# A linear-attention layer and a feed-forward layer in one kernel: weight transfers tied to loads, two small inputs spread by TensorE, filler matmuls, and a new instruction order

## The chip, the cores and the metric

The kernel runs on one core of a Trainium2 chip. The metric is the device time of one execution in microseconds (us); the median over the runs is compared. Profiles are of single executions, and their span runs from the first to the last instruction of the program.

## The reference: what is computed

Four sequences of 768 steps with 8 heads of width 48 go through a recurrence, and its output goes through a feed-forward layer.

```python
for t in range(S):                       # S = 768, per batch b and head h
    cur = outer(u * k[t], v[t])
    y[t] = r[t] @ (state + cur)          # state is 48 x 48
    state = w[:, None] * state + outer(k[t], v[t])
x = y.transpose(0, 2, 1, 3).reshape(3072, 384)
h = x @ w_in                             # 384 x 2048
g = where(h >= 1, h, where(h <= -1, 0, (h + 1) ** 2 / 4))
out = g @ w_out                          # 2048 x 384
```

All inputs and the output are float32. `w` and `u` have 8 x 48 entries.

## The kernel before, in words

**Units and blocks.** The recurrence is cut into chunks of 128 steps. Six chunks times four sequences give 24 *units*; unit `i` is chunk `i // 4` of sequence `i % 4`. Two units make one *block* of 256 rows for the feed-forward layer, 12 blocks in all.

**One unit of the attention part.** Three loads bring K, R and V of the unit, each 128 x 384 float32 (L250, on SP's queue, tokens `ld:K:i` and so on). K and R are scaled by powers of `w` into one tile RKW (`Kw:i`, `Rw:i`, L254). The tile is transposed, for units 0 to 7 by TensorE (`trp:i`, L278, with the copy `trc:i`), for the others by a transposing DMA on SP's queue (`tr:i`, L287). Scores follow on TensorE (`at:i`, L294) and are masked on VectorE (`mk:i:s`, L298). The diagonal term needs K times u times R (`KU1:i` L262, `KU2:i` L265), a row sum (`dg:i`, L269) and, for units 0 to 5, V times that sum (`VD:i`, L273). `Vb:i` is V in bf16. `y:i` (L306 to L315) is the output in PSUM, `x:i` its copy, `xs:i` a sum of squares of it (L344), and `xp:i` its transposition, by TensorE for units 0 to 7 (L334, then the copy `xT:i`) and by DMA otherwise (L340). `st:i` (L350) is the unit's contribution to the state; `Ta`, `Td` and `Tb` (L356, L358, L361, L180) add, decay and cast the state. The decay uses the column vector `wc`.

**One block of the feed-forward part.** `L1:m:n` (L373) is six matmuls of 256 columns, 0.66 us; blocks 0 and 1 are worked unit by unit instead (`L1:m:n:u`, twelve matmuls of 128 columns, 0.67 us) so that they can begin with one finished unit. `sm:m:n` (L384, ScalarE) applies the quadratic. `L2:m:u:n` (L400) is two matmuls of 384 columns, 0.33 us. `oc:m:u` copies the result out of PSUM and `so:m:u` stores it (L415, SP's queue).

**Weights.** `w_in` and `w_out` are cast from float32 to bf16 while they are loaded, so POOL issues them, each in four quarters: `gi:q` (L422) and `go:q` (L425). `li:q` and `lo:q` stand for their landings. `L1` with index `n` of blocks 0 and 1 needs quarter `n` of `w_in`; `L2` with index `n` needs quarter `n // 2` of `w_out`.

**The order.** A string `ORDER`, found by a search ahead of time, lists every operation once as a token. The program walks through it and emits each operation on its engine, so the string fixes the order within every engine and within every DMA queue; nothing is reordered across a wait. A token `KU2:3@DVE` overrides the engine. The durations in the `op(...)` table were used by the search; in the kernel itself only the engine, the emitting function and the choice count.

**Small inputs.** `u` is loaded into all 128 rows by a broadcast DMA (L228), `w` likewise (L225), and `wc` by two DMAs of single words (L233), which stand in SP's queue between `ld:R:1` and `ld:K:2`.

Of the kernel before, what the change touches and what calls it, by code (L numbers as in the profile page):

```python
# [16 lines left out]
w ld:K:0 u gi:0 ld:R:0 ln tab:K ld:K:1 tab:R Kw:0 ld:V:0 gi:1 ld:V:1 Rw:0 li:0 trp:0 gi:2 trc:0 KU1:0 at:0  # L17
KU2:0 li:1 mk:0:1 gi:3 mk:0:0 dg:0 Vb:0 ld:R:1 VD:0 st:0 Kw:1 y:0 wc x:0 li:3 KU1:1 xs:0 xp:0 Rw:1 xT:0 dec
KU2:1 trp:1 Ta:0:1 L1:0:0:0 ld:K:2 trc:1 Ta:0:0 Vb:1 dg:1 L1:0:1:0 ld:R:2 VD:1 sm:0:0:0 st:1 go:1 sm:0:1:0
Ta:1:1 at:1 li:2 Ta:1:0 L1:0:3:0 Tb:0:1 Kw:2 mk:1:0 Tb:0:0 Tb:1:1 mk:1:1 sm:0:3:0 KU1:2 Tb:1:0 ld:V:2 Rw:2  # L20
y:1 KU2:2 x:1 ld:R:3 xs:1 trp:2 go:0 dg:2 L1:0:2:0 ld:K:3 trc:2 xp:1 Vb:2 ld:V:3 sm:0:2:0 VD:2 go:3 xT:1
at:2 ld:K:4 st:2 mk:2:1 go:2 L1:0:1:1 ld:V:4 Ta:2:0 L1:0:0:1 Rw:3 sm:0:1:1 lo:0 Kw:3 Ta:2:1 Tb:2:0 L1:0:2:1
mk:2:0 sm:0:0:1 KU1:3 Tb:2:1 L1:0:3:1 sm:0:2:1 y:2 Kw:4 ld:R:4 trp:3 x:2 trc:3 KU2:3@DVE ld:R:5 dg:3 KU1:4
xp:2 L2:0:1:0 sm:0:3:1 lo:1 L2:0:0:0 Rw:4 L2:0:0:1 xT:2 L2:0:1:1 Vb:4 xs:2 at:3 KU2:4 L1:1:0:0 mk:3:1 trp:4
ld:K:5 VD:3 sm:1:0:0 L1:1:2:0 mk:3:0 Vb:3 trc:4 ld:V:5 L1:1:1:0 dg:4 sm:1:2:0 st:4 VD:4 ld:R:6 y:3 Kw:5
Ta:4:1 sm:1:1:0 L2:0:1:2 Ta:4:0 at:4 ld:K:6 x:3 st:3 Rw:5 L1:1:3:0 xs:3 KU1:5 mk:4:0 ld:V:6 L2:0:0:2
sm:1:3:0 xp:3 Ta:3:1 L2:0:1:3 KU2:5 xT:3 mk:4:1 lo:2 L2:0:0:3 trp:5 Tb:3:1 Ta:3:0 Td:4 trc:5 dg:5 L1:1:0:1
Vb:5 y:4 VD:5 sm:1:0:1 lo:3 L1:1:2:1 Kw:6 x:4 at:5 Tb:4:1 Rw:6 sm:1:2:1 L1:1:1:1 mk:5:1 xs:4 xp:4 KU1:6
mk:5:0 st:5 L1:1:3:1 ld:R:7 xT:4 Ta:5:0 sm:1:1:1 trp:6 KU2:6 Ta:5:1 ld:K:7 y:5 sm:1:3:1 L2:0:0:4 Td:5 Tb:4:0
dg:6 ld:V:7 L2:0:1:4 x:5 Vb:6 L2:0:0:5 Tb:3:0 L2:0:1:5 trc:6 ld:R:8 L2:0:1:6 xp:5 st:6 Rw:7 L2:0:0:6 Ta:6:1  # L30
xT:5 ld:K:8 L2:0:0:7 Ta:6:0 L2:0:1:7 Tb:5:1 oc:0:0 Kw:7 at:6 Tb:5:0 ld:V:8 xs:5 oc:0:1 L1:2:0 Td:6 mk:6:0
L2:1:0:0 ld:K:9 sm:2:0 L2:1:0:1 KU1:7 mk:6:1 trp:7 ld:R:9 L1:2:2 KU2:7 trc:7 L1:2:4 ld:V:9 Vb:7 sm:2:2 y:6
dg:7 Vb:8 L2:2:1:0 Tb:6:0 x:6 so:0:0 L1:2:1 Kw:8 sm:2:4 so:0:1 at:7 sm:2:1 ld:R:10 L2:1:0:2 Rw:8 mk:7:1
Tb:6:1 st:7 L1:2:3 xs:6 ld:K:11 Ta:7:1 KU1:8 xp:6 Ta:7:0 sm:2:3 L2:1:0:3 mk:7:0 L2:1:0:4 ld:V:10 xT:6 KU2:8
L1:2:5 st:8 L2:1:0:5 sm:2:5 tr:8 Td:7 y:7 dg:8 Kw:9 L2:1:0:6 x:7 Tb:7:0 L2:1:0:7 Tb:7:1 ld:R:11 L1:2:6 Rw:9
L1:2:7 sm:2:6 ld:K:12 Ta:8:1 Vb:9 L2:2:1:1 oc:1:0 sm:2:7 xp:7 KU1:9 ld:K:10 Ta:8:0 L2:2:1:2 xs:7 L2:1:1:0
L2:1:1:1 Td:8 xT:7 ld:V:11 L2:1:1:2 KU2:9 L2:1:1:3 L2:1:1:4 L2:1:1:5 tr:9 L2:1:1:6 Vb:10 dg:9 at:8 Rw:10
L1:3:3 ld:R:12 mk:8:1 L1:3:0 Kw:10 sm:3:3 mk:8:0 ld:V:12 st:9 L2:1:1:7 sm:3:0 Ta:9:1 Rw:11 L2:2:1:3 oc:1:1
L1:3:1 ld:V:13 Ta:9:0 Kw:11 y:8 sm:3:1 so:1:0 L1:3:2 x:8 Tb:8:1 tr:10 Td:9 st:10 L1:3:4 sm:3:2 KU1:11 Tb:8:0
at:9 Ta:10:0 so:1:1 sm:3:4 L2:2:1:4 KU1:10@DVE ld:R:13 L1:3:5 xs:8 mk:9:1 KU2:10 L2:2:1:5 sm:3:5 ld:K:13  # L40
L1:3:6 mk:9:0 Vb:11 L2:2:1:6 Ta:10:1 sm:3:6 xp:8 L1:3:7 KU2:11 dg:10 y:9 sm:3:7 tr:11 L2:2:1:7 Td:10 x:9
st:11 Rw:12 oc:2:1@ACT at:10 Tb:9:0 L2:2:0:0 ld:K:14 Tb:9:1 L2:2:0:1 Kw:12 dg:11 L2:2:0:2 xs:9 L2:2:0:3
ld:R:14 mk:10:0 L2:2:0:4 KU1:12 L2:2:0:5 mk:10:1 L2:2:0:6 xp:9 L2:2:0:7 KU2:12 Ta:11:1 L2:3:1:0 oc:2:0
L2:3:1:1 ld:V:14 y:10 Vb:12 Ta:11:0 L2:3:0:0 x:10 Tb:10:0 Kw:13 L2:3:0:1 so:2:1 Tb:10:1 at:11 tr:12 L2:3:1:2
Vb:13 L2:3:0:2 Rw:13 mk:11:1 L2:3:0:3 xs:10 L2:3:1:3 so:2:0 mk:11:0 L2:3:1:4 ld:K:15 Rw:14 L2:3:0:4 st:12
dg:12 L2:3:0:5 L1:4:0 xp:10 Ta:12:1 Td:11 Ta:12:0 Kw:14 y:11 sm:4:0 ld:R:15 L1:4:1 x:11 Tb:11:1 Td:12 L1:4:2
sm:4:1 ld:V:15 KU1:14 L2:3:1:5 sm:4:2 L1:4:3 tr:13 KU1:13 Tb:11:0 at:12 sm:4:3 L1:4:4 mk:12:0 KU2:13 xs:11
xp:11 L1:4:5 mk:12:1 sm:4:4 KU2:14 L2:3:0:6 ld:K:16 dg:13 sm:4:5 L2:3:1:6 L1:4:6 Vb:15@ACT Vb:14 ld:R:16
dg:14 y:12 Rw:15 sm:4:6 L1:4:7 x:12 ld:V:16 Tb:12:0 L2:3:1:7 Kw:15 sm:4:7 L2:3:0:7 st:13 tr:14 st:14
oc:3:0@ACT oc:3:1 KU1:15 at:13 Tb:12:1 Ta:13:0 xs:12 L2:4:0:0 mk:13:1 ld:K:17 L1:5:0 KU2:15 mk:13:0 L2:4:1:0  # L50
sm:5:0 xp:12 L1:5:1 Kw:16 Ta:13:1 L2:4:1:1 Ta:14:1 sm:5:1 so:3:1 L1:5:2 Ta:14:0 Rw:16 dg:15 so:3:0 y:13
sm:5:2 ld:R:17 L2:4:0:1 Td:13 x:13 L1:5:3 Td:14 Tb:13:0 ld:V:17 L2:4:1:2 Vb:16 sm:5:3 at:14 Kw:17 L2:4:0:2
# [46 lines left out]
def kernel(  # L99
# [11 lines left out]
    nc = tc.nc  # L111
# [24 lines left out]

# [499 lines left out]
```

## Time and profile before

| | us |
|---|---|
| Median of 14 runs | 191.56 |
| Lowest and highest run | 190.12, 193.16 |
| The profiled execution's own time | 191.57 |
| Its span | 189.8 |
| TensorE busy | 161.3 |
| VectorE, ScalarE, GpSimd busy | 117.6, 108.1, 114.4 |

The profile's page has the busy time of each engine, the span in 40 slices, the DMA queues, the chain of waits that ended last, and the groups of instructions. Its names are PE for TensorE (PEld for its weight loads), DVE for VectorE, ACT for ScalarE, POOL for GpSimd and SP for the engine that issues most DMAs; "SPq" is SP's queue. `L254` is line 254 of the kernel. In a line of the timeline the two first numbers are the start and the duration in us, and a bracket at the end says how long the engine was idle before and what ended that. Matmuls overlap in the pipeline, so their busy time is a little more than what they cost.

### The profile page before, as it was taken

Reading aid. Unit: us, or ns where it says so; the run is one execution under the profiler, and the core shown is the slowest. Engines: PE = TensorE matmul, PEld = TensorE weight load, DVE = VectorE, ACT = ScalarE, POOL = GpSimd, SP = SyncE. Lnnn points to the kernel's source line nnn. Section 1 sums busy time; section 2 is a strip of 40 time slices with the busy share of each in tenths; the row PEclk is TensorE's granted clock in tenths of the full one; section 3 lists DMA queues with packets and bytes.
Section 4 is the critical chain, followed back from the end, with each engine's and each line's share of the span. In section 5 each row is a group of like instructions: output and inputs, shape, how many; then the busy total and the mean of one; then the engine's idle time right before and its main releaser. Section 6 shows DMA issues by size and latency. Waiting matters only on the chain.

```text
span 189.8 us, 4565 instructions
## 1 busy us (share of the span) xinstructions
PE 161.3 (85%) x1728; PEld 122.2 (64%) x1728; DVE 117.6 (62%) x312; ACT 108.1 (57%) x227; POOL 114.4 (60%) x151
## 2 busy tenths in 40 slices
PE   0214669789999999999999999998699999999980
PEld 0102648578877777667877767675477777777750
DVE  2240699698578568987886958959479746011210
ACT  3313475896978637439766576483876544643310
POOL 8744799099689898999988759883960000000000
PEclk9999996999999999999999999999999999999998
DMA  4999999999948999898989999989894112120031
GB/s 95 189 207 201 179 190 199 191 182 207 166 118 147 189 218 191 168 218 172 155 201 186 150 220 195 161 197 181 176 240 99 32 24 83 21 83 3 10 111 62
DMA packets 106476, 28.55 MB, mean 150 GB/s; under 512 B 99408, under 2 KB 106448, under 8 KB 106448
## 3 DMA queue, kind: packets, MB, share of 16 engines
q1 hardware_dynamic: 102592, 24.95, 68.1%
q0 software_dynamic: 3712, 3.15, 10.6%
q8 instruction: 15, 0.25, 0.5%
q14 instruction: 13, 0.11, 0.2%
q10 hardware_dynamic: 144, 0.10, 0.2%
HBM read 20.84 MB, written 4.72 MB: 135 GB/s over the span
## 4 chain that ended last, share of the span: by engine, by line
PE 60%; DMA 13%; DVE 9%; POOL 6%; SPq 5%; ACT 2%; issue 2%; ACTq 0%; DVEq 0%; POOLq 0%
PE o_p L400 26%; PE h_p L373 24%; DMA K<-in_k_dram 5%; DMA R<-in_r_dram 4%; POOL RKW L254 4%; DVE VD L273 4%; DMA wc<-in_w_dram 3%; PE A L294 3%; DVE AT L298 2%; PE y L309 2%; SPq L287 2%; PE y L306 1%; SPq L340 1%; PE tr L278 1%; DVE RKW L254 1%
## 5 line engine op out<-in xcount | busy, mean ns | idle before, releaser
L384 ACT ACTIVATE gT<-h_p 128x512 bf16<-128x512 f32 x96 | 56.9, 596 | 40.4 <-PE h_p L373 39.4
L373 PE MATMUL h_p<-xT,w_in_sb 128*128 128x256 bf16 (+1 forms) x672 | 78.8, 263 | 1.2 <-ACT gT L384 1.1
L400 PE MATMUL o_p<-w_out_sb,gT 128*128 128x384 bf16 (+1 forms) x400 | 76.4, 320 | 2.3 <-ACT o_sb L180 2.2
L373 PEld LDWEIGHTS <-w_in_sb 128*128 128x128 bf16 x672 | 58.9, 101 | 13.1 <-issue 1.5
L400 PEld LDWEIGHTS <-gT 128*128 128x128 bf16 x400 | 36.2, 98 | 18.0 <-issue 2.7
L298 DVE TENSOR_TENSOR AT<-A,umask 128x512 bf16<-128x512 f32 x48 | 31.4, 682 | 7.6 <-PE A L294 7.4
L326 DVE SCALAR_TENSOR_TENSOR x<-Vb,dg,y 128x48 bf16<-128x48 bf16 x144 | 26.8, 259 | 10.1 <-PE y L309 10.1
L265 POOL TENSOR_TENSOR KU<-KU,R 128x384 f32<-128x384 f32 x23 | 23.9, 1042 | 10.6 <-DMA R<-in_r_dram 8.3
L254 POOL TENSOR_TENSOR RKW<-K,Winv 128x384 bf16<-128x384 f32 x24 | 24.6, 1027 | 5.5 <-DMA K<-in_k_dram 4.6
L262 POOL TENSOR_TENSOR KU<-K,u_bc 128x384 f32<-128x384 f32 x22 | 22.3, 1016 | 2.2 <-DMA K<-in_k_dram 2.2
L180 ACT CAST Tbd<-T 48x192 bf16<-48x192 f32 x40 | 13.9, 349 | 10.5 <-POOL T L361 5.9
L180 DVE COPY o_sb<-o_p 128x384 f32<-128x384 f32 x20 | 10.9, 553 | 14.4 <-PE o_p L400 14.2
L269 DVE TENSOR_REDUCE dg<-KU 128x8 f32<-128x384 f32 x24 | 13.1, 547 | 9.8 <-POOL KU L265 9.7
L254 POOL TENSOR_TENSOR RKW<-R,Wpow 128x384 bf16<-128x384 f32 x18 | 18.0, 1001 | 1.9 <-DMA R<-in_r_dram 1.8
L278 PE MATMUL tr<-ident,RKW 128*128 128x128 bf16 x64 | 6.5, 247 | 11.9 <-POOL RKW L254 7.0
L344 ACT ACTIVATE x<-x 128x384 bf16<-128x384 bf16 x24 | 12.5, 520 | 2.3 <-DVE x L326 2.0
L356 DVE TENSOR_TENSOR T<-T,st 48x192 f32<-48x192 f32 x32 | 11.2, 351 | 3.4 <-PE st L350 2.6
L278 PEld LDWEIGHTS <-RKW 128*128 128x128 bf16 x64 | 4.7, 109 | 13.0 <-POOL RKW L254 7.0
L180 POOL CAST Vb<-V 128x384 bf16<-128x384 f32 x22 | 11.4, 519 | 2.4 <-DMA V<-in_v_dram 2.4
L273 DVE TENSOR_TENSOR VD<-V,dg 128x384 bf16<-128x384 f32 x6 | 10.8, 1806 | 1.2 <-DMA V<-in_v_dram 1.1
L294 PE MATMUL A<-RK 48*128 48x128 bf16 x192 | 10.2, 229 | 1.3 <-ACT RK L180 1.1
L254 DVE TENSOR_TENSOR RKW<-R,Wpow 128x384 bf16<-128x384 f32 x6 | 4.6, 763 | 10.9 <-DMA R<-in_r_dram 10.9
(56 smaller groups left out, 122.1 us busy)
## 6 DMA issues: line engine op xcount, KB each, us to landing
K<-in_k_dram SPq DMA_DIRECT2D x24, 192.0 KB, 4.0
R<-in_r_dram SPq DMA_DIRECT2D x24, 192.0 KB, 3.9
V<-in_v_dram SPq DMA_DIRECT2D x24, 192.0 KB, 4.5
out_dram<-o_sb SPq DMA_DIRECT2D x23, 192.0 KB, 2.2
w_in_sb<-in_moe_w_in_dram POOLq DMA_DIRECT2D x4, 384.0 KB, 7.9
w_out_sb<-in_moe_w_out_dram POOLq DMA_DIRECT2D x4, 384.0 KB, 7.2
RK<-RKW SPq DMA_TRANSPOSE x16, 3.6
xT<-x SPq DMA_TRANSPOSE x16, 2.9
```

Of the source, the lines that this page charges most:

```text
L180: (eng.copy if eng is nc.scalar else eng.tensor_copy)(to, src)
L254: at_engine((name + "w", i)).tensor_mul(RKW[i % RING["W"]][:, off : off + H, 0:D], t[name, i], tab)
L262: at_engine(("KU1", i)).tensor_mul(t["KU", i], t["K", i], u3)
L265: at_engine(("KU2", i)).tensor_mul(t["KU", i], t["KU", i], t["R", i])
L269: nc.vector.reduce_sum(t["dg", i], t["KU", i], axis=AX)
L273: at_engine(("VD", i)).tensor_mul(t["VD", i], t["V", i], t["dg", i][:, :, None].to_broadcast([128, H, D]))
L294: mm(t["A", i][s][:, p, :], KT[rows[s], p, :], RT[rows[s], p, :], start=True, stop=True)
L298: nc.vector.tensor_mul(t["AT", i, s], t["A", i][s], umask4)
L326: nc.vector.scalar_tensor_tensor(x[:, h * D : (h + 1) * D], t["Vb", i][:, h, :], t["dg", i][:, h : h + 1], t["y", i][:, h, :], op0=ALU.mul ...
L373: mm(h_p[:, f, :], w_in_sb[:, kk, (nf * n + f) * 128 : (nf * n + f + 1) * 128], xT[m][:, :, kk, :] if u_ is None else xT[m][:, u_, kk, :], ...
L384: nc.scalar.activation(g, h_p, AF.Square, bias=0.5, scale=0.5)
L400: mm(t["o", m, u, part_], t["g", m][:, f, u * C : (u + 1) * C], w_out_sb[:, f, e], start=(f == 0), stop=(f == nN - 1),)
```

## The change

Five things change together.

1. Each of the eight weight transfers is preceded on POOL by a copy of one element of a named load into a scratch tile, so POOL issues the transfer only after that load has landed. `w_in` is held by K1, R1, V1 and K2, `w_out` by K3, R3, V3 and K4 (the number is the unit).
2. `u` is loaded as one row of 384 words. A float32 matmul with a column of ones spreads it over 128 rows in PSUM (`ub`), and a copy (`uc`) brings it to SBUF.
3. The two word-wise DMAs of `wc` are gone. Eight small matmuls turn the logarithm of `w` from a row into columns (`wt`), and two exponentials make `wc` of it.
4. Tokens `warm*N` emit N matmuls of the 128 x 128 identity into unused columns of an output bank; there are 161 of them, all but six ahead of the first matmul of unit 4. They are not waited for by anything.
5. The order is another one. Among other things SP's queue loads V0 ahead of R0 and V2 ahead of K1, unit 4 goes ahead of unit 3, several operations change engine (`Kw:2`, `trc:0`, `KU1:1` and others to VectorE, `Rw:2`, `Rw:3` to GpSimd), and the later units' attention stands further behind relative to the feed-forward matmuls.

The diff, cut to its core; of the two orders only the first lines are shown:

```diff
 ORDER = """
-w ld:K:0 u gi:0 ld:R:0 ln tab:K ld:K:1 tab:R Kw:0 ld:V:0 gi:1 ld:V:1 Rw:0 li:0 trp:0 gi:2 trc:0 KU1:0 at:0
-KU2:0 li:1 mk:0:1 gi:3 mk:0:0 dg:0 Vb:0 ld:R:1 VD:0 st:0 Kw:1 y:0 wc x:0 li:3 KU1:1 xs:0 xp:0 Rw:1 xT:0 dec
-KU2:1 trp:1 Ta:0:1 L1:0:0:0 ld:K:2 trc:1 Ta:0:0 Vb:1 dg:1 L1:0:1:0 ld:R:2 VD:1 sm:0:0:0 st:1 go:1 sm:0:1:0
...
+w u ld:K:0 ld:V:0 ln warm*12 ub tab:K ld:R:0 tab:R Kw:0 wt uc ld:V:2 dec KU1:0 ld:K:1 Rw:0 KU2:0 ld:R:1
+warm*30 trp:0 Vb:0 ld:K:2 dg:0 gi:0 warm*7 st:0 trc:0@DVE ld:V:1 Ta:0:1 gi:1 warm*6 at:0 Ta:0:0 Tb:0:1
+mk:0:1 ld:R:2 gi:3 mk:0:0 li:0 Kw:1 Tb:0:0 VD:0 Rw:1 warm*44 y:0 Kw:2@DVE trp:1 li:1 x:0 Rw:2@POOL xs:0 xp:0
+xT:0 gi:2 warm*3 trp:2 trc:1 L1:0:0:0 Vb:1 li:3 Vb:2 sm:0:0:0 KU1:1@DVE warm*7 at:1 trc:2 st:1 KU2:1 mk:1:0
+L1:0:1:0 Ta:1:1 li:2 st:2 KU1:2 sm:0:1:0 mk:1:1 Tb:1:1 dg:1 KU2:2 warm*10 at:2 Ta:1:0 L1:0:3:0 mk:2:1 Tb:1:0
+ld:K:3 sm:0:3:0 VD:1 mk:2:0 ld:R:3 dg:2 warm*17 y:1 L1:0:2:0 VD:2 ld:R:4 x:1 go:0 Ta:2:0 xs:1 Ta:2:1 ld:K:4
+sm:0:2:0 warm*6 y:2 KU1:3 xp:1 x:2 xT:1@DVE ld:V:3 Tb:2:1 go:1 Tb:2:0 warm*13 xp:2 xs:2 lo:0 L1:0:1:1 Rw:4
+Kw:4 L1:0:0:1 sm:0:1:1 sm:0:0:1 L1:0:3:1 go:2 xT:2 L1:0:2:1 lo:1 KU1:4 sm:0:3:1 trp:4 sm:0:2:1 L1:1:0:0
+KU2:4 trc:4 L2:0:0:0 L1:1:1:0 go:3 ld:V:4 dg:4 sm:1:0:0 L2:0:1:0 L2:0:1:1 sm:1:1:0 Kw:3 ld:K:6 L1:1:2:0 at:4
+Rw:3@POOL sm:1:2:0 lo:2 L1:1:3:0 mk:4:0 Vb:3 sm:1:3:0 mk:4:1 L2:0:1:2 KU2:3 L2:0:1:3 trp:3 L2:0:0:1 VD:4
...
+    u_row = const.tile([1, H * D], F32, name="u_row")
+    onef = const.tile([1, 128], F32, name="onef")
+    nc.vector.memset(onef, 1.0)
+    hold = const.tile([1, 2 * NQ], F32, name="hold")
...
+    def warm(count):
+        if spare[0] is None and ("o", 0, 0, None) not in t and ("o", 0, 1, None) not in t:
+            spare[0] = ps_o.tile([128, 512], F32, name="w_p", tag="o")
+            mm(spare[0][:, d_out:], ident, ident, start=True, stop=False, skip_group_check=True)
+        if spare[0] is not None:
+            for i in range(count):
+                mm(spare[0][:, d_out:], ident, ident, start=False, stop=False, skip_group_check=True)
...
     def load_u():
-        nc.sync.dma_start(out=u_bc, in_=row_bcast(u))
-
-    def load_wc():
-        with nc.allow_non_contiguous_dma(reason="384 words"):
+        nc.sync.dma_start(out=u_row, in_=bass.AP(tensor=u.tensor, offset=u.offset, ap=[[0, 1], [1, H * D]]))
+
+    def spread_u():
+        t["u"] = ps_a.tile([128, H * D], F32, name="u_p", tag="a")
+        mm(t["u"], onef, u_row, start=True, stop=True)
...
+    def turn_w():
+        t["wp"] = ps_a.tile([128, NP], F32, name="w_p", tag="a")
+        for p in range(NP):
             for s in range(2):
-                nc.sync.dma_start(out=wc[rows[s], :], in_=w.rearrange("(p s) d -> s d p", s=2)[s])
+                h = 2 * p + s
+                mm(t["wp"][rows[s], p : p + 1], lw[0:1, h * D : (h + 1) * D], onef[0:1, 0:1], start=True, stop=True)
...
     def decay():
-        nc.scalar.activation(wc, wc, AF.Ln)
-        nc.scalar.activation(wc, wc, AF.Exp, scale=float(C))
+        for s in range(2):
+            nc.scalar.activation(wc[rows[s]], t["wp"][rows[s]], AF.Exp, scale=float(C))
...
-    def load_in(q):
-        nc.gpsimd.dma_start(out=w_in_sb[:, :, q * FQ : (q + 1) * FQ], in_=w_in_src[:, :, q * FQ : (q + 1) * FQ])
+    IN = [(0, 1, "K1"), (1, 2, "R1"), (2, 3, "V1"), (3, 4, "K2")]
+    OUT = [(0, 1, "K3"), (1, 2, "R3"), (2, 3, "V3"), (3, 4, "K4")]
...
+    def wait_for(j, f):
+        nc.gpsimd.tensor_copy(hold[0:1, j : j + 1], t[held(f)][0:1, 0, 0:1])
+
+    def load_in(z):
+        a, e, f = IN[z]
+        wait_for(z, f)
+        nc.gpsimd.dma_start(out=w_in_sb[:, :, a * FQ : e * FQ], in_=w_in_src[:, :, a * FQ : e * FQ])
```

Two orders of single queues matter below. POOL before unit 5 in the new order: `Kw:0 KU1:0 KU2:0 Vb:0 gi:0 gi:1 gi:3 Kw:1 Rw:2 gi:2 Vb:1 Vb:2 KU2:1 KU1:2 KU2:2 go:0 KU1:3 go:1 Kw:4 go:2 KU1:4 KU2:4 go:3 Kw:3 Rw:3 Vb:3 KU2:3`. SP's queue in the new order: `w u K0 V0 R0 V2 K1 R1 K2 V1 R2 K3 R3 R4 K4 V3 V4 K6 K5 R5 ...` up to V8, and then the first store.

## The prediction

> **What bounds the kernel now.** I read the page's slices first, then PE by windows, then the chain and the timeline at the places where PE is idle, and last SP's queue. Page and windows (columns: stretch, length, busy us and counts of PE, PEld, DVE, ACT, POOL, then PEclk, DMA share, GB/s):
>
> ```profile
> PE   0214669789999999999999999998699999999980
> DMA  4999999999948999898989999989894112120031
> ```
> ```profile
> 0.00:36.00 36.00, 16.48 (x195) 13.57 (x196) 20.41 (x33) 15.53 (x31) 25.30 (x42) 0.95 1.10 181
> 36.00:50.00 14.00, 13.04 (x212) 10.85 (x210) 10.85 (x21) 11.94 (x26) 10.69 (x12) 1.00 1.04 188
> 50.00:120.00 70.00, 70.00 (x752) 52.12 (x750) 53.42 (x167) 46.70 (x105) 62.06 (x78) 1.00 0.97 178
> 120.00:130.00 10.00, 9.78 (x97) 7.08 (x96) 7.51 (x21) 6.70 (x15) 6.96 (x9) 1.00 0.90 191
> 130.00:140.00 10.00, 7.70 (x77) 5.51 (x76) 7.08 (x19) 6.29 (x14) 8.31 (x11) 1.00 0.98 205
> 140.00:184.00 44.00, 44.00 (x410) 33.06 (x408) 18.31 (x55) 20.31 (x40) 1.08 (x2) 1.00 0.21 57
> ```
>
> PE is never idle from 50 to 120 and from 140 to 184. What can move is the start (19.5 us idle before 36), a dip around 132, and the fixed end (last matmul at 184.27, span 189.8: 5.5 us).
>
> So I keep a ledger of PE. Full-speed costs from the chain: L1 of 256 columns 0.655, of 128 columns 0.67, L2 0.326, `at` 0.36, `y` 0.36 (0.53 with VD), `st` 0.17, `trp` 0.45, `xp` 0.17. Sums: L1 10.7 + 52.4, L2 62.6, `at` 8.6, `y` 9.7, `st` 3.4, `trp` 3.6, `xp` 1.4, norm 0.4: 152.8 us, the same in both orders. The *offset* of a matmul is its start less the work listed ahead of it. `L1:1:0:0` has 12.5 ahead and starts at 38.42: offset 25.9. The end has 152.8 ahead and comes at 184.27: 31.5. The growth of 5.5 is 3.5 us of idle after 36 (the windows: 0.96 + 0.22 + 2.30) and 2.0 of small losses. Chain, in order of time:
>
> ```profile
> 38.42 0.78 PE h_p L373 x12
> ...
> 177.39 6.88 PE o_p L400 x58
> ```
>
> *Why the offset is 26.* Timeline:
>
> ```profile
> 19.98 0.56 DVE L254 TENSOR_TENSOR RKW<-R,Wpow 128x384 bf16<-128x384 f32 x1 [5.39 <-DMA R<-in_r_dram]
> 20.60 0.61 PE L278 MATMUL tr<-ident,RKW 128*128 128x128 bf16 x4 [3.75 <-DVE RKW L254]
> 21.00 2.77 PE L373 MATMUL h_p<-xT,w_in_sb 128*128 128x128 bf16 x24
> 28.43 4.41 DVE L273 TENSOR_TENSOR VD<-V,dg 128x384 bf16<-128x384 f32 x1
> ```
>
> x0 is ready at 16.9, but `L1:0:0:0` stands behind `trp:1`, which needs R1. R1 was issued at 8.79 and took 11.2 us to land (the answer for tile R at that window), since the four `w_in` quarters are in flight from about 6 to 19. Landings in the trace: R0 7.03, K1 10.97, V0 13.6, V1 19.3, R1 20.0, then R3 at 23.8; with `w_out` in flight V3 28.4, K4 29.2, V4 30.3, R4 37.6. Alone, loads land 0.9 us apart. [...]
>
> *Why there is a dip at 132.*
>
> ```profile
> 127.14 0.57 SPq L250 DMA_DIRECT2D K<-in_k_dram  x1
> 131.17 1.00 POOL L254 TENSOR_TENSOR RKW<-K,Winv 128x384 bf16<-128x384 f32 x1 [3.58 <-DMA K<-in_k_dram]
> 134.52 0.48 PE L400 MATMUL o_p<-w_out_sb,gT 128*128 128x384 bf16 x2 [2.19 <-ACT o_sb L180]
> ```
>
> K22 is issued late, `Kw:22` waits, `Td:18` stands behind it on POOL, `Tb:18` behind that, the PSUM copy `oc:6:0` behind that on ACT, and PE waits for the bank. SP's queue issues with little idle (7 of 81 us) from `tr:8` at 58.82 to `tr:23` at 140.17. The old order has 34.9 and 110.0 us of PE work ahead of these two, 75.1 between, and SP needs 81.35: its lag behind the listed place grows from 23.9 to 30–31, past PE's 26.
>
> **The change, part by part.**
>
> *Small inputs.* Removed: the 192 KB broadcast of `u` (one load's worth of engine time, 0.9 us; 0.57 of SP) and the word-wise `wc` (2.95 + 1.83 us of SP, and it lands at 20.3, where `Ta:0` waits). Added: `ub`, by the float32 row (272 ns for 128 columns) 0.8, at most 1.3; `wt`, eight small matmuls by the norm's row (163 ns) at most 1.3, at least 0.4; `uc` 0.48 (row of x<-y); `dec` 0.2 + 0.2. All lie between 4.2 (w and u land) and 6.9 where PE and ACT are idle; without that cover, 2–3 us ahead of `trp:0`. V0 takes u's place among the transfers, so R0 still lands at 7.0.
>
> *Holds.* Eight one-element copies: by the nearest POOL rows 0.1 (memset) to 0.3 us (identf), I take 0.1; each `gi`/`go` still issues for 0.75–0.94. What they cost is what queues behind the wait on POOL: behind `gi:2` Vb1, Vb2, KU2:1; behind `go:2` (V3) KU1:4, KU2:4, `go:3`, Kw:3, Rw:3 and so `trp:3`.
>
> [...] By the landings above, the order decides: six small loads ahead of the weights land 0.9 apart and not 3 to 6. [...]
>
> *Filler matmuls.* 161 of 128 columns: 55 ns each at full speed (0.67 / 12), 115 at the early speed (2.77 / 24), so 8.9 to 18.5 us of PE's queue. Before `trp:4` stand 155 of them and 10.4 of work: 21 us warm, 30 cold with `ub` and `wt`, and by the replay below `trp:4` cannot start before 31.5. So I book 0; all cold they would cost up to 3. What is their use? [...] The trace shows PE busy 16.5 us by 36 for 9.7 of listed work, 6.8 lost in all, as its gaps keep it slow. But that excess lies mostly in time when PE would wait for loads, so it goes into the replay and not on top.
>
> *Start replayed with the trace's durations.* Landings 0.9 apart after R0: V2 7.95, K1 8.85, R1 9.8, K2 10.7, V1 11.6. POOL: Kw:0 5.9–6.9, KU1:0, KU2:0 to 9.4 (Rw:0 on DVE gets between them and ends at 8.5, as before), Vb:0 9.9, `gi:0`, `gi:1`, `gi:3` to 13.0; Kw:1 14.1. Weights flow from 12 on, 2.87 us a quarter at 82%: 14.9, 17.7, 20.6. R2 needs its last half load at 18%: 14.8; Rw:2 15.8; `gi:2` 16.9, landing 23.5. DVE: dg 10.0, trc 10.7, Ta, masks 12.7, VD:0 13.5, Rw:1 14.5. `y:0` 13.6, xT:0 16.0, `trp:2` 16.3, `L1:0:0:0` 16.3 (before 21.0); the last of unit 0's four at 23.6 (before 28.4).
> Next, K3 at 19.8 and R3 at 24.5; POOL Vb, KU2:1, KU1:2, KU2:2 to 20.9, `go:0` 21.9, KU1:3, `go:1` 25.5; quarters land at 26.4 and 29.9. K4 follows at 30.3, V3 31.2. Kw:4 31.3, `trp:4` 31.5 with 10.4 ahead: offset 21.1. `go:2` 32.3, KU1:4, KU2:4, `go:3` 35.3, Kw:3, Rw:3 37.3, `trp:3` 37.4 with 15.5 ahead: 21.9. `go:3` lands at 39.6, and `L2:0:0:6` with 19.65 ahead then has 20. VD:3 meets a train of POOL work, as the VD of 4.41 us above did, so I add 0.4: **offset 22.3**, 3.6 less than 25.9.
>
> *Later.* The first store came at 53.86 with 30.7 ahead, 2.8 inside PE's offset; with 30.8 ahead it may now come at 50, and V8, one load less, lands by 49. `tr:8` was 2.0 inside the offset; now, with 38.2 ahead, it comes at 58.5, lag 20.3. `tr:23` has 118.2 ahead, 80.0 between, for the same 12 transposes of x and 15 of RK, two loads less and two stores more. At 81.35 SP's lag ends at 21.7, just under 22.3: the wait on K22 is gone. I take off the 2.3 idle of 130–140, and keep the other 1.2 and 2.0. Next late would be x at the end: from `xp:22` to its L1 the list has 7.2 (11.5 before), for a landing of 3.9.
>
> *Sum* for the profiled execution: 152.8 + 22.3 + 3.1 = 178.2 for the last matmul, + 5.5 = 183.7 span, + 1.8 outside it (191.57 against 189.8) = 185.5 us. That execution stands at the median, 191.56.
>
> **The rivals.**
> - *Only half of it* (188.5; 187 to 190.5): the dip stays because SP's transposes slow down when DMA is busier (their issues ran from 1.2 to 3.2 us), 185.5 + 2.3; or K4 comes 3 us later. For it: the DMA row stands at 8 or 9 tenths for three quarters of the span. Against: the new list leaves SP 5 us more.
> - *Bytes decide*: 191.6 - 0.9 = 190.7, up to 192. For it: DMA is full from 2 to 45. Against: at 40 PE has done 14 us of work (offset 26), where the six units landed by then hold 6 x 6.3.
> - *Slower: the hold of `go:2` on V3.* If V3 fares as R4 did before (12.6 us to land, the usual 3.9: 8.7 later), POOL stands, Kw:3 and Rw:3 move by as much, `trp:3` starts at 46.1 with offset 30.6, and the time is 191.6 + (30.6 - 25.9) - 2.3 = 194.0. It turns slower where V3 lands after 37.5, 6.3 later than replayed. For it: loads crawl beside weights, and a hold on a crawling load delays the next weights. Against: between `go:1` and `go:2` nothing else is in flight, so the loads run alone.
> - *It doesn't do what it says*: the holds, if the loads had landed anyway. But K1 lands at 8.85 and the old `gi:0` began at 4.08, so they act.
>
> **How the numbers follow.** Main case 0.55 (185.5, alone 182 to 188; best, with an offset of 19, 181.5), half 0.17, bytes 0.08, slower 0.20 (193 to 197). This kernel's measurement tells about 0.5%, 1 us, from no change. Faster: 0.55 + 0.17 + 0.01 = 0.73; within: the rest of bytes, 0.07; slower 0.20. Range 181 to 193.5: it leaves out some 0.04 below and 0.14 above.
>
> **What would show it.** Right: R1 landing near 10; `L1:0:0:0` near 16.3; `trp:4` near 31.5; `L1:1:0:0` with offset 21–22; no wait of over 1 us on K in POOL after 100; no `wc` wait on ACT. Wrong: POOL waiting over 3 us at a hold while PE idles, filler matmuls running when the next real operand is ready, `trp:3` after 43, or a PE window after 50 with over 1 us idle.

## The result, and the profile after

The changed kernel takes 186.31 us, the median of 10 runs (184.15 to 188.67), beside 191.39 us for the kernel before (189.98 to 193.67): a ratio of 0.968, 95% interval 0.964 to 0.972. The forecast was 185.5. The profiled execution took 186.99 us with a span of 185.1. The ratio is taken from the faster runs of the changed kernel (184.15 to 186.9 us), while every trace of it below is of a slower one (186.6 to 187.8 us), so the losses that its traces show may be smaller in its fastest runs.

Page of the changed kernel, PE, its clock and the DMA engines in 40 slices:

```profile
PE   5999699949999999999999999999999999999980
...
PEclk9999999996999999999999999999999999999996
...
DMA  3999999989993569579988998898997421310131
```

PE's early slices are full because idle matmuls count as busy. Two things answer to the lines of before: the slices at 132 us are now nines, and there is a new weak place, in PE in the ninth slice (37 to 42 us) and in its clock in the tenth (42 to 46 us). The same by windows (stretch, length, busy us and counts of PE, PEld, DVE, ACT, POOL, then PEclk, DMA share, GB/s):

```profile
0.00:36.00 36.00, 31.82 (x451) 27.51 (x452) 18.65 (x39) 19.37 (x40) 27.31 (x52) 1.00 1.07 184
36.00:50.00 14.00, 11.20 (x109) 7.26 (x107) 12.17 (x16) 5.48 (x13) 10.17 (x12) 0.88 1.01 198
...
120.00:130.00 10.00, 10.00 (x110) 7.71 (x109) 9.29 (x24) 8.46 (x19) 7.07 (x7) 1.00 0.93 173
130.00:140.00 10.00, 10.00 (x106) 7.46 (x102) 8.73 (x26) 7.05 (x16) 7.64 (x11) 1.00 0.94 201
```

Where before had 2.30 us of idle PE between 130 and 140 there is none. Between 36 and 50, where before had 0.96, there are 2.80, and 12% of the clock was not granted (0.12 x 14 = 1.7 us).

In the ledger of the prediction (offset = start of a matmul less the work listed ahead of it), before against after: 25.8 against 19.4 at `L1:1:0:0`; 26.7 against 24.9 at `L1:1:3:1`, the next block-1 matmul behind unit 3; 28.2 to 30.9 across block 8 against 26.1 throughout; 31.5 against 26.8 at the end. So a lead of 6.4 us at the start of block 1 shrinks to 1.8 within 19 us, and the dip gives 2.7 back. The start, in the timeline:

```profile
9.25 0.18 POOL L460 COPY hold<-K 1x1 f32<-1x1 f32 x1
9.38 0.94 POOL L465 DMA_DIRECT2D w_in_sb<-in_moe_w_in_dram  x1
16.81 0.83 PE L401 MATMUL h_p<-xT,w_in_sb 128*128 128x128 bf16 x12
19.57 0.84 PE L401 MATMUL h_p<-xT,w_in_sb 128*128 128x128 bf16 x12 [0.94 <-DMA w_in_sb<-in_moe_w_in_dram]
24.69 0.17 POOL L460 COPY hold<-R 1x1 f32<-1x1 f32 x1 [2.80 <-DMA R<-in_r_dram]
29.82 0.61 PE L306 MATMUL tr<-ident,RKW 128*128 128x128 bf16 x8
```

`L1:0:0:0` starts at 16.81 (21.00 before). The hold of the first quarter has no bracket: POOL arrived at it directly from `Vb:0`, and K1 had landed at 8.81. The same is true of all four holds of `w_in`. Of the eight, only `go:1`'s waited in this trace, 2.80 us for R3.

The place where the lead is lost, at 35 to 42:

```profile
34.98 4.54 DVE L301 TENSOR_TENSOR VD<-V,dg 128x384 bf16<-128x384 f32 x1
36.70 0.49 POOL L182 CAST Vb<-V 128x384 bf16<-128x384 f32 x1
37.16 0.99 POOL L282 TENSOR_TENSOR RKW<-K,Winv 128x384 bf16<-128x384 f32 x1
38.12 0.98 POOL L290 TENSOR_TENSOR KU<-K,u_bc 128x384 f32<-128x384 f32 x1
39.57 0.32 PE L343 MATMUL y<-VD,ident 128*128 128x384 bf16 x1 [1.63 <-DVE VD L301]
41.26 0.39 PE L322 MATMUL A<-RK 48*128 48x128 bf16 x7 [0.89 <-DVE T L386]
41.59 1.94 PE L432 MATMUL o_p<-w_out_sb,gT 128*128 128x384 bf16 x6
```

`VD:4` is a product that takes 0.56 us where nothing keeps it out, as `VD:3` does at 40.02 in this trace. Here it takes 4.54 and ends at 39.52, 0.42 after POOL's train of products ends (38.12 + 0.98 = 39.10). `y:4` waits 1.63 for it, the state update behind it on VectorE is late and `at:3` waits 0.89. After these gaps PE's clock is halved from 41.8 to 45.2 (0.50 granted there, 1.00 from 36.0 to 41.8): six matmuls take 1.94 us, where six cost 3 x 0.326 = 0.98 at full speed. This is one execution; in the traces of two more runs of the same kernel (below) the loss is smaller and the clock is whole.

### The profile page after: what moved, and what is told of

The parts are those of the page before. It is cut to its first block, busy times and chain, and to the rows that moved or that the text cites. A ratio compares the mean times of both kernels' runs of the same rounds, so it can differ in the third digit from the quotient of the medians.

```text
span 185.1 us, 4923 instructions
## 1 busy us (share of the span) xinstructions
PE 172.6 (93%) x1906; PEld 132.2 (71%) x1906; DVE 124.3 (67%) x327; ACT 106.6 (58%) x225; POOL 107.3 (58%) x148
## 4 chain that ended last, share of the span: by engine, by line
PE 79%; DMA 8%; POOL 5%; DVE 2%; issue 2%; ACT 1%
PE o_p L432 34%; PE h_p L401 34%; DMA w_in_sb<-in_moe_w_in_dram 6%; PE A L322 4%; PE y L337 2%; DMA w_bc<-in_w_dram 2%; PE y L334 2%; POOL RKW L282 2%; PE st L378 1%; POOL w_in_sb L465 1%; PE tr L306 1%; DVE VD L301 1%; PE xp L362 1%; POOL KU L293 1%; PE w_p L240 1%
## 5 line engine op out<-in xcount | busy, mean ns | idle before, releaser
L401 PE MATMUL h_p<-xT,w_in_sb 128*128 128x256 bf16 (+1 forms) x672 | 74.4, 257 | 1.9 <-DMA w_in_sb<-in_moe_w_in_dram 1.8
L432 PE MATMUL o_p<-w_out_sb,gT 128*128 128x384 bf16 (+1 forms) x400 | 75.4, 324 | 0.2 <-DVE o_sb L182 0.2
L401 PEld LDWEIGHTS <-w_in_sb 128*128 128x128 bf16 x672 | 56.3, 98 | 12.7 <-DMA w_in_sb<-in_moe_w_in_dram 2.4
L354 DVE SCALAR_TENSOR_TENSOR x<-Vb,dg,y 128x48 bf16<-128x48 bf16 x144 | 26.7, 257 | 9.3 <-PE y L337 8.5
L290 POOL TENSOR_TENSOR KU<-K,u_bc 128x384 f32<-128x384 f32 x22 | 22.3, 1014 | 6.7 <-DMA K<-in_k_dram 6.7
L282 POOL TENSOR_TENSOR RKW<-K,Winv 128x384 bf16<-128x384 f32 x21 | 22.0, 1049 | 6.8 <-DMA K<-in_k_dram 5.2
L182 ACT CAST Tbd<-T 48x192 bf16<-48x192 f32 x40 | 13.9, 347 | 18.7 <-DVE T L386 9.4
L293 POOL TENSOR_TENSOR KU<-KU,R 128x384 f32<-128x384 f32 x18 | 18.6, 1036 | 1.2 <-DVE KU L290 0.5
L240 PE MATMUL w_p<-ident 128*128 128x128 bf16 x155 | 13.2, 250 | 0.0
L389 POOL TENSOR_TENSOR T<-T,wc 128x192 f32<-128x192 f32 x16 | 8.1, 507 | 8.1 <-DVE T L384 3.4
L240 PEld LDWEIGHTS <-ident 128*128 128x128 bf16 x159 | 11.8, 114 | 0.2
L182 POOL CAST Vb<-V 128x384 bf16<-128x384 f32 x19 | 10.0, 531 | 1.4 <-DMA V<-in_v_dram 1.0
L322 PEld LDWEIGHTS <-RK 48*128 48x128 bf16 x192 | 5.5, 94 | 6.3 <-issue 4.6
```

What stands on the lines that cost most here:

```text
L182: (eng.copy if eng is nc.scalar else eng.tensor_copy)(to, src)
L240: mm(spare[0][:, d_out:], ident, ident, start=False, stop=False, skip_group_check=True)
L282: at_engine((name + "w", i)).tensor_mul(RKW[i % RING["W"]][:, off : off + H, 0:D], t[name, i], tab)
L290: at_engine(("KU1", i)).tensor_mul(t["KU", i], t["K", i], u3)
L293: at_engine(("KU2", i)).tensor_mul(t["KU", i], t["KU", i], t["R", i])
L322: mm(t["A", i][s][:, p, :], KT[rows[s], p, :], RT[rows[s], p, :], start=True, stop=True)
```

## The experiments

The kernels ran in three groups, each beside the kernel before: `e1` to `e4` (median of before 193.38 us), then `a0`, `e3b`, `b1` and `b3` (192.99), then, on another chip, `a1`, `c1`, `b4` and `b5` (192.63). So ratios to before are compared across groups, and medians only within one. The changed kernel itself ran again in the second and in the third group, as `a0_changed` and `a1_changed`.

> The changed kernel again, unedited, beside the kernels of this call on the same chip. Both theories: 0.965 to 0.975 of the kernel before. A second profile shows whether VD:4 is kept out by POOL in each execution: my theory is that it is a matter of a few hundred ns which of the two gets in first, so the time of VD:4 and the offset at L1:1:3:1 (25 us in the first profile) may differ by 2 to 3 us between executions.

> The changed kernel again, unedited, to stand beside the next kernel on the same chip: 184 to 189 us on two levels, ratio about 0.96 to 0.97.

Measured: 186.99 us (183.6 to 192.11), ratio 0.955 (0.941 to 0.968), and 186.39 us (183.52 to 189.66), ratio 0.958 (0.950 to 0.965). `VD:4` is kept out in each of the three traces, for 3.71 and 2.77 us in these two. The loss from `L1:1:0:0` to `L1:1:3:1` is 3.3 us (20.4 to 23.7) and 2.3 us (20.4 to 22.7), where the first trace has 5.5; the granted clock between 36 and 50 is 1.00 in both, so of these three the first alone has the halved clock.

### Late weights: undone, and done alone

`e4_weights_early`, the changed kernel with `w_in` issued as early as before:

```diff
-warm*30 trp:0 Vb:0 ld:K:2 dg:0 gi:0 warm*7 ... gi:1 ... ld:R:2 gi:3 ... xT:0 gi:2
+ld:R:0 tab:R gi:0 Kw:0 gi:1 gi:2 ... KU2:0 gi:3 ld:R:1 warm*30 trp:0 Vb:0
...
     def load_in(z):
         a, e, f = IN[z]
-        wait_for(z, f)
```

> The changed kernel with the w_in transfers issued as early as in the kernel before (ahead of and between Kw:0 and KU2:0) and without their holds; everything else stays. My theory: the loads of units 0 to 2 crawl beside the weights again, R1 or R2 lands after 17, L1:0:0:0 starts at 20 to 22, offset at unit 4 back to 22 or more, time 187 to 190. Rival (bytes decide, the order of landing does not): time within 0.5% of the changed kernel.

Measured: 194.69 us (193.82 to 195.99), ratio 1.012 (1.005 to 1.019): slower than before, and more than expected.

```profile
4.08 0.94 POOL L462 DMA_DIRECT2D w_in_sb<-in_moe_w_in_dram  x1
21.93 0.99 POOL L280 TENSOR_TENSOR RKW<-R,Wpow 128x384 bf16<-128x384 f32 x1 [8.26 <-DMA R<-in_r_dram]
23.38 1.49 PE L399 MATMUL h_p<-xT,w_in_sb 128*128 128x128 bf16 x12
34.34 6.83 DVE L280 TENSOR_TENSOR RKW<-R,Wpow 128x384 bf16<-128x384 f32 x1
41.23 0.40 PE L304 MATMUL tr<-ident,RKW 128*128 128x128 bf16 x4 [3.43 <-DVE RKW L280]
```

R2, which the new order needs for `trp:2` ahead of `L1:0:0:0`, lands at 21.86 behind the quarters, and POOL stands 8.26 us: `L1:0:0:0` at 23.38 with an offset of 20.8 for 14.2. Then comes a second loss that the edit did not intend: `Rw:4` on VectorE is shut out by a POOL train for 6.83 us and PE waits 3.43 for it; offset 30.6 at `L1:1:0:0`. The changed kernel's own trace loses 5.5 at `VD:4` after that place, and at the end the two are about as far apart as at the start (33.5 and 26.8). So the 6.6 us at the start are the price of early weights in these traces, and the rival, that only bytes decide, is refuted.

`b1_weights_late`, the kernel before with the four `gi` tokens moved behind `Vb:0`:

```diff
-w ld:K:0 u gi:0 ld:R:0 ... ld:V:0 gi:1 ... trp:0 gi:2 ... mk:0:1 gi:3 mk:0:0 dg:0 Vb:0
+w ld:K:0 u ld:R:0 ... ld:V:0 ... trp:0 ... mk:0:1 mk:0:0 dg:0 Vb:0 gi:0 gi:1 gi:2 gi:3
```

> The kernel before with one edit: the four w_in transfers are issued by POOL behind Vb:0 instead of around Kw:0 and KU1:0. My theory: K1 to R1 land by about 11 to 13 instead of 11 to 20, L1:0:0:0 starts at 16.5 to 18.5 instead of 21.0, the offset at L1:1:0:0 falls from 25.8 to 22.5 to 24.5, the dip at 132 stays; time 188 to 190.5 where before is 191.4 (1 to 2% less). Rival (old order cannot use it, VD and the w_out quarters set the pace): within 0.5% of before or slower.

Measured: 194.29 us (193.03 to 196.79), ratio 1.007 (1.002 to 1.012). The gain expected did not come.

```profile
17.02 0.80 POOL L423 DMA_DIRECT2D w_out_sb<-in_moe_w_out_dram  x1
22.98 1.48 POOL L423 DMA_DIRECT2D w_out_sb<-in_moe_w_out_dram  x2
33.81 0.99 POOL L252 TENSOR_TENSOR RKW<-K,Winv 128x384 bf16<-128x384 f32 x1 [9.36 <-DMA K<-in_k_dram]
```

`L1:0:0:0` does start at 16.8. But POOL is now ahead and issues `w_out` between 17.0 and 23.7 (21.8 to 27.8 before), straight behind `w_in`, and K3 crawls: issued at 13.14, landed at 33.74. The wait moved from R1 to K3. `b4_both_late` therefore moves `w_out` as well:

```diff
-... Vb:0 gi:0 gi:1 gi:2 gi:3 ... go:1 ... KU2:2 ... go:0 ... Vb:2 ... go:3 ... go:2 ... KU1:3 ... KU1:4
+... Vb:0 gi:0 gi:1 gi:2 gi:3 ... KU2:2 go:1 ... Vb:2 go:0 ... KU1:3 go:3 ... KU1:4 go:2
```

> The kernel before, its searched order kept, but with both kinds of weight transfer issued later by their place in POOL's order: the four w_in quarters after Vb:0 (as in b1_weights_late), and the four w_out quarters after KU2:2, Vb:2, KU1:3 and KU1:4, where POOL cannot pass before K3 and K4 are there. Nothing else of the change is in it. Theory: b1_weights_late gained nothing because an idle POOL then issued w_out at 17.0 to 23.7 us, and K3, V3 and R3 lay behind it until 33.7 to 37.3 us (POOL waited 9.36 us for K3). With w_out apart, K3 lands by about 26 us, L1:1:0:0 starts with an offset of about 22 to 23 us where before has 25.8, the dip at block 8 stays, and the time is 187 to 189.5 us where before has 191.5 (ratio 0.98 to 0.99). Rival: the late weights pay only in an order searched for them; then POOL's later products miss their units as VD:3 and VD:4 do in the changed kernel, the offset at L1:1:3:1 is 26.5 us or more and the time 191 us or over.

Measured: 191.16 us (189.77 to 191.77), ratio 0.989 (0.982 to 0.996). K3 lands at 26.89, the offset is 23.2 at `L1:1:0:0` and 23.6 at `L1:1:3:1`, close to the theory's 22 to 23. The ratio is at the upper end of the theory's 0.98 to 0.99 (its 187 to 189.5 us were for a before of 191.5). The dip is still there, as it said, and a little larger, 27.2 to 30.5 across block 8:

```profile
129.50 1.00 POOL L252 TENSOR_TENSOR RKW<-K,Winv 128x384 bf16<-128x384 f32 x1 [2.81 <-DMA K<-in_k_dram]
133.21 0.59 PE L398 MATMUL o_p<-w_out_sb,gT 128*128 128x384 bf16 x2 [1.78 <-ACT o_sb L178]
```

`b5_both_late_small` adds the small inputs:

```diff
-... tab:R Kw:0 ... y:0 wc x:0
+... tab:R ub wt uc Kw:0 ... y:0 x:0
```

> As b4_both_late, and the small inputs as in the changed kernel: u spread and w turned by TensorE in place of the two broadcast loads and the two loads of wc, no holds, no fillers. Theory: these four transfers stand among the first twelve of SP's queue, where the two loads of wc took 0.87 and 0.44 us of issue and lay between R1 and K2 in b1_weights_late; without them R1, K2 and the quarters come about 1 us earlier, and the offset is 0.5 to 1 us under that of b4_both_late: 186.5 to 189 us, 0.3 to 0.5% under it. Rival: the first products wait for the chain from u's row through TensorE to the spread copy, and nothing is gained: the time is that of b4_both_late or up to 1 us above it.

Measured: 188.79 us (188.08 to 189.95), ratio 0.980 (0.973 to 0.987), 1.2% under `b4_both_late` by medians of one chip; more than expected. Most of the difference is not at the start: the offsets at `L1:1:0:0` are 23.1 and 23.2. The traces part later, by 0.5 us at `L1:1:3:1`, by 1.8 us at block 6, by 1.1 at the start of block 8 and by 2.8 behind the step there, which is 1.6 and not 3.3. Why four transfers at the start should tell so late was not settled. `b5_both_late_small` also has the changed kernel's wider PSUM tile for the output (512 columns for 384), whose part was not measured.

### Holds and idle matmuls taken out

`e2_no_hold` and `e1_no_fill`:

```diff
     def load_in(z):
         a, e, f = IN[z]
-        wait_for(z, f)
...
-        wait_for(NQ + z, f)
```

> The changed kernel without the eight one-element copies; order and fillers stay. My theory: in the trace the four w_in holds found their loads already landed and only go:1 waited (2.8 us for R3), so the place of the issues in POOL's order does the work. L1:0:0:0 near 16.8, go:1 issued near 22, K4 one to three us later, time within 1% of the changed kernel (184.5 to 187). Rival (the holds are the gain): w_in goes out earlier, R1 or K2 land after 14, time 189 or above.

```diff
         if token.startswith("warm"):
-            warm(int(token[5:]))
             continue
```

> The changed kernel without its 161 filler matmuls. My theory: the gain at the start comes from the order of the transfers, so landings do not move and L1:0:0:0 still starts near 16.8; TensorE then runs at half rate through the early gaps, so unit 1's 48 matmuls take 5.5 instead of 3.0 us and trp:4 comes 2 to 3 us later, but y:4 waits for VD:4 until 39.5 anyway. Time 185 to 187, at most 1% above the changed kernel. Rival (the fillers are the gain): TensorE stays slow until after 45, the offset at block 2 rises by 3 us or more, time 188.5 or above.

Measured: without holds 185.33 us (181.93 to 187.23), ratio 0.948 (0.939 to 0.956); without fillers 186.77 us (184.77 to 187.72), ratio 0.965 (0.957 to 0.973). Neither is slower than the changed kernel (0.955 to 0.968 in its three comparisons).

The holds do move something, though it isn't worth time. Timeline of `e2_no_hold`:

```profile
21.73 0.81 POOL L468 DMA_DIRECT2D w_out_sb<-in_moe_w_out_dram  x1
30.18 0.98 POOL L282 TENSOR_TENSOR RKW<-K,Winv 128x384 bf16<-128x384 f32 x1 [7.64 <-DMA K<-in_k_dram]
```

Without the hold on R3, `go:1` goes at 21.73 and not at 24.81, and K4 lands 1.7 us later, at 30.1; `trp:4` starts at 31.2 for 29.8. The `w_in` quarters go as before, behind `Vb:0`. And of the fillers, timeline of `e1_no_fill`:

```profile
15.69 1.49 PE L401 MATMUL h_p<-xT,w_in_sb 128*128 128x128 bf16 x12
18.35 0.84 PE L401 MATMUL h_p<-xT,w_in_sb 128*128 128x128 bf16 x12 [0.25 <-DMA w_in_sb<-in_moe_w_in_dram]
```

The first twelve matmuls run at half speed (1.49 for 0.83), and PE still waits for the next quarter of weights afterwards. The half speed costs nothing there. `L1:1:0:0` comes at 28.97, earlier than with fillers (30.27).

### The dip at block 8

`b3_k22_early`, the kernel before with two loads earlier in SP's queue:

```diff
-... xp:16 ... ld:K:22 ... ld:R:22
+... ld:K:22 ld:R:22 xp:16
```

> The kernel before with one edit: the loads K22 and R22 stand ahead of xp:16 on SP's queue instead of behind xp:17, some five places earlier. My theory: K22 is issued near 121 to 122 instead of 127.1, Kw:22 does not wait, the step of the offset by 2.7 us between L1:8:1 and L1:8:2 goes, time 1 to 1.5% below before. Rival (SP is simply late by then, and the wait moves to K23 or to the transposes of RK): the step returns within 10 us, time within 0.5% of before.

Measured: 193.39 us (192.07 to 193.9), ratio 0.999 (0.995 to 1.003): nothing gained. POOL no longer waits for K22, and the step at block 8 is gone (32.5 to 32.6). But this trace loses as much and more a block earlier, where PE waits for a transposition of x:

```profile
119.88 1.46 PE L372 MATMUL h_p<-xT,w_in_sb 128*128 128x256 bf16 x6 [2.92 <-DMA xT<-x]
```

The offset rises from 27.9 to 32.3 around `L1:7:0`, and the six matmuls behind the wait run at half speed (1.46 us, 0.82 for six of the same shape at 115.98). The edit did not make this wait: the transposition, `xp:15`, was issued at 114.40 (112.62 before), and the moved loads only at 123.89 and 124.93, behind it. So the trace cannot tell what an earlier K22 is worth. Ten runs say that it is worth nothing that shows in the time; why stays open.

How did the change get rid of the dip, then? Not by an earlier K22, as the timeline of the changed kernel shows:

```profile
130.10 0.50 POOL L389 TENSOR_TENSOR T<-T,wc 128x192 f32<-128x192 f32 x1
130.55 0.50 POOL L182 CAST Vb<-V 128x384 bf16<-128x384 f32 x1
132.91 0.99 POOL L290 TENSOR_TENSOR KU<-K,u_bc 128x384 f32<-128x384 f32 x1 [1.86 <-DMA K<-in_k_dram]
```

POOL still waits 1.86 us for K22 (3.58 before). But in the old order `Td:18`, the decay of the state, stood behind `Kw:22` on POOL, and the copy `oc:6:0`, which frees PE's bank, behind `Tb:18` on ACT. The new order breaks this chain in two places: `Td:18` and `Td:19` come ahead of the first product with K22, and `oc:6:0` is on VectorE. The traces of all kernels agree. In the nine with the new order POOL waits 1.86 to 3.70 us for K22, and the offset in block 8 moves by no more than 0.1; in the four with the old order and a wait of 2.22 to 3.58 us (before, `b1`, `b4`, `b5`) it steps by 1.6 to 3.3. The old order with only these tokens moved was not run, so which of the two places does it, and what it is worth in time, is not shown.

The new order has a wait of the same kind elsewhere. `sm:7:2` stands on ACT behind the cast of V20, and in three of its nine traces (`a1`, `e1`, `c1`) V20 is late and PE waits 0.84 to 1.76 us for it ahead of block 8. From `a1_changed`:

```profile
122.29 0.51 ACT L182 CAST Vb<-V 128x384 bf16<-128x384 f32 x1 [1.84 <-DMA V<-in_v_dram]
123.35 1.47 PE L401 MATMUL h_p<-xT,w_in_sb 128*128 128x256 bf16 x12 [1.04 <-ACT gT L412]
```

### VD:4 and VD:3 let through

`e3_let_vd4_pass` makes POOL wait for `VD:4` by a copy of one of its elements ahead of `KU2:3`; `e3b_let_vd34_pass` does so for `VD:3` too, ahead of `Kw:6`:

```diff
+    def let_pass(i):
+        nc.gpsimd.tensor_copy(hold[0:1, 2 * NQ + i : 2 * NQ + i + 1], t["VD", i][0:1, 0, 0:1])
...
-mk:4:1 L2:0:1:2 KU2:3 L2:0:1:3 trp:3 L2:0:0:1 VD:4 trc:3 ... VD:3 Kw:6
+mk:4:1 VD:4 yv:4 L2:0:1:2 KU2:3 L2:0:1:3 trp:3 L2:0:0:1 trc:3 ... VD:3 yv:3 Kw:6
```

In `e3_let_vd4_pass`, `yv:3` is not there.

> The changed kernel with VD:4 moved directly behind unit 4's masks in the list (its place on VectorE is the same) and a one-element copy of its result put into POOL's order ahead of KU2:3, so that POOL pauses until VectorE's two-input product is through. My theory: VD:4 took 4.54 us because POOL's products kept it out; now under 1.5 us, y:4 does not wait, TensorE does not fall idle around 38 to 41 and is not throttled around 42 to 45; offset at block 2 near 21 to 22.5 instead of 25.0, time 181 to 183.5. Rival (y:4 and what follows would wait for w_out or for the scores of unit 3 anyway): at most 1 us gained, 184.5 to 186.

Measured: 188.13 us (184.92 to 188.62), ratio 0.973 by medians: no gain, since the changed kernel has 0.973, 0.969 and 0.968 by medians. `VD:4` took 0.99 us, but now `VD:3` met the train, 2.16 us, and `at:3` waited for the state update behind it:

```profile
38.13 2.16 DVE L300 TENSOR_TENSOR VD<-V,dg 128x384 bf16<-128x384 f32 x1
40.99 0.61 PE L321 MATMUL A<-RK 48*128 48x128 bf16 x7 [1.62 <-DVE T L385]
```

> The changed kernel with one-element copies that make POOL wait for VD:4 and also for VD:3 (the first alone moved the block to VD:3, 2.16 us, whose Ta:3 and Ta:4 held a PSUM bank that at:3 needs). My theory: both products are through by 39, at:3 starts at 39.5 to 40 instead of 41, TensorE is not throttled, offset at L1:1:3:1 22 to 23.5 instead of 24.6 to 25, time 1.0 to 1.5% below the changed kernel on this chip. Rival (the last w_out quarters, which land at 39.5 to 40.4, end the wait anyway): offset stays above 24, time within 0.5% of the changed kernel.

Measured: 184.59 us (184.26 to 185.81), ratio 0.954 (0.945 to 0.964), 1.3% under `a0_changed` by medians.

```profile
34.36 1.09 DVE L300 TENSOR_TENSOR VD<-V,dg 128x384 bf16<-128x384 f32 x1
35.77 0.18 POOL L472 CAST hold<-VD 1x1 f32<-1x1 bf16 x1
37.52 0.56 DVE L300 TENSOR_TENSOR VD<-V,dg 128x384 bf16<-128x384 f32 x1
38.14 0.18 POOL L472 CAST hold<-VD 1x1 f32<-1x1 bf16 x1 [0.79 <-DVE VD L300]
```

`VD:3` was let through by the wait. `VD:4` was not: it got in by itself, between `Rw:3` and `Vb:3` on POOL, and had ended (35.45) before POOL came to the copy, which therefore has no bracket; so it was in `e3_let_vd4_pass`. Both products are short, the clock is not halved, and the offset at `L1:1:3:1` is 21.0 for 24.9; the span is 182.9.

`c1_pass_no_hold_no_fill` takes the same wait into the kernel without holds and fillers (the three diffs above together).

> The changed kernel without its eight holds and without its idle matmuls, and with POOL waiting for VD:4 and VD:3 before it goes on with KU2:3 and with the products behind VD:3, as in e3b_let_vd34_pass. Theory: holds and fillers are worth nothing that can be measured (e1_no_fill, e2_no_hold), and the wait keeps VD:4 and VD:3 at 1 to 2 us each, so the offset at L1:1:3:1 is about 21 us as in e3b_let_vd34_pass and the time 183 to 185.5 us without an upper level, 1 to 1.5% under a1_changed. Rival: without fillers TensorE's clock is halved in the gap before L1:1:3:1 in some executions, and the time is 186 to 188 us.

Measured: 184.91 us (183.54 to 187.34), ratio 0.957 (0.951 to 0.962), beside 186.39 and 0.958 for `a1_changed`. Here POOL waits at both copies (3.96 and 0.79 us), `VD:4` takes 0.55, `VD:3` 0.56, and there are 1.4 us of loss from `L1:1:0:0` to `L1:1:3:1` where the changed kernel's three traces lose 5.5, 3.3 and 2.3. But in its trace R2 landed at 17.75 and `L1:0:0:0` started at 19.3, and it lost 2.1 more ahead of block 8, at the late V20. The two kernels that let VD pass are 1.3 and 0.8% under the changed kernel by medians and equal to it by the ratios (0.954 against 0.955, 0.957 against 0.958). So a version that beats it is not shown.

## Why the prediction was right, point by point

- **The landings** (right, most within two microseconds, `trp:3` 2.4 off): R1 9.65 (predicted 9.8), K2 10.50 (10.7), `w_in` at 16.1, 19.5, 22.1, 24.5 (14.9, 17.7, 20.6, 23.5), K3 18.7 (19.8), R3 24.6 (24.5), K4 28.4 (30.3), V3 29.2 (31.2). `L1:0:0:0` at 16.81 (16.3), `trp:4` at 29.82 (31.5), `trp:3` at 35.0 (37.4). No run shows the replay's 2.87 us a weight quarter at 82%, or the 18% for R2, which were the author's estimates: the quarters of `w_in` landed 3.42, 2.53 and 2.42 us apart here, 3.85, 2.45 and 2.56 in the kernel before (10.18, 14.03, 16.48, 19.04), and R2 landed at 12.36 (14.8).
- **"The order decides, not the bytes"** (right): by the rival "bytes decide" the gain was 0.9 us; it was 0.032 x 191.4 = 6.1 by the ratio and 5.1 by the medians. `b4_both_late`, which moves no byte less than before, gains 1.1%, and `e4_weights_early` loses all of the gain.
- **"So they act"** (wrong): the holds did not do it. The step compared K1's landing with the *old* place of `gi:0`. In the new order `gi:0` stands behind `Vb:0`, and POOL comes to it at 9.25, after K1. The place in POOL's order does the delaying, and `e2_no_hold` shows it by leaving the holds out. The rival "it doesn't do what it says" was true of the `w_in` holds, and cost nothing.
- **VD, "so I add 0.4"** (wrong in size, the largest error): from `trp:3` to `L1:1:3:1` the offset grew by 5.4 in the first trace, with 2.8 of idle PE between 36 and 50 and 1.7 of ungranted clock in it; the two repeats lose 3.3 and 2.3 in block 1. The 4.41 us of a VD in the trace of before was the warning; it was booked at what it cost *there*, not at what it costs with PE's next work behind it.
- **"Offset 22.3"** (wrong): 19.5 at `trp:3` and not 21.9, then 24.9. At `L1:1:0:0`, where the sign of being right was 21 to 22, it was 19.4.
- **"The wait on K22 is gone"** (the gain right, the step wrong): SP took 87.1 us from `tr:8` to `tr:23` (56.04 to 143.11) and not 81.35, and its lag did not fall to 21.7 but ended at 24.9. K22 was issued at 129.88 and POOL waited 1.86 us, against "no wait of over 1 us on K in POOL after 100". The step in the offset went all the same, since the decay of the state no longer stood behind that wait and the copy of the bank no longer behind the decay. That the booked 2.3 us came by another path is luck.
- **Fillers at 0** (right), shown by `e1_no_fill`: without them the first twelve matmuls of `L1` took 1.49 us for 0.83, and PE waited for weights behind them all the same (0.25 us), as the replay had it. The sign against it came true at no cost in time: the operand of `trp:0` was ready at 8.00 and `trp:0` started at 8.94 behind the fillers (7.82 without them).
- **Small inputs** (under-sized, as far as one run says): booked at about 0.9 us of transfers inside the replay; beside `b4_both_late` they brought 2.4 us by medians, though not at the start, and the cause is open. `ub` took 1.61 us, more than the 1.3 allowed, and ACT did not wait for `wc`, as forecast.
- **The sum**: last matmul at 179.59 (178.2), that is 2.6 more in the front and 1.2 less later (1.9 for 3.1); the tail of 5.5 as before, 1.9 outside the span. Two errors at the front of 2.4 down and 5.0 up stand behind a total that is 1.5 off for the profiled execution and 0.8 for the median; that they cancel in part is luck.

## What to carry to other kernels

Small loads that the first matmuls need go ahead of bulky transfers (R1 landed at 9.65 us here, 19.96 before), and the place of the bulky ones in their issuing queue was enough for that (`e2_no_hold`, ratio 0.948); but when one transfer is delayed, look which next one its queue then issues earlier (in `b1_weights_late` `w_out`, at 17.0 us for 21.8). When a late load stalls an engine in program order, look at what stands behind its wait: here the wait stayed (1.86 us, 3.58 before), and with nothing urgent behind it the matmuls no longer felt it, though this was not tried by itself. And a short product of two SBUF tensors on VectorE that met a train of products on POOL took until the end of the train in six traces here, 2.77 to 6.83 us for 0.56; book it at up to what is left of the train, and ask what waits behind it.

## What the runs showed of the hardware

A product of two SBUF tensors on VectorE that met a train of products on POOL was kept out to the end of the train in six traces. `VD:4` ended 0.42 us after POOL's last product in the changed kernel (39.52 and 39.10), and likewise in `e1_no_fill` (38.44 and 38.02), in `a0_changed` (39.72 and 39.30), `a1_changed` (38.72 and 38.31) and `e2_no_hold` (40.92 and 40.50), and `Rw:4` in `e4_weights_early` (41.17 and 40.75): 2.77 to 6.83 us for a product of 0.56. It is not always so: in the same trace of the changed kernel `Rw` of a later unit got in after one product of POOL. It started at 46.15, POOL's product ended at 46.99, and it ended at 47.41, again 0.42 later, while POOL's next product took 1.33 us for 1.00. When it gets in stays open.

The load R2, issued 0.3 to 0.9 us ahead of the first quarter of `w_in`, landed at 12.36, 14.03, 15.64 and 17.75 us (changed kernel, `a0_changed`, `a1_changed`, `c1_pass_no_hold_no_fill`; issued at 8.58, 8.41, 8.54, 9.11). A small load just ahead of a large one took 3.8 us in one run and 8.6 in another. Whether this, or the VD, makes the times of the runs differ stays open.
